# An attention and two-MLP kernel: one weight tile converted at each step of the second phase, low parts on VectorE

## The chip, the cores and the metric

The kernel runs on one core of a Trainium2 chip. A core has TensorE (PE; its weight loads are shown as PEld), VectorE (DVE), ScalarE (ACT), GpSimd (POOL) and SyncE (SP), which here only issues DMAs. The metric is the device time of one execution in microseconds (us), the median of several runs.

## What is computed

```python
def _attn_ref(q, k, v, s):                      # q, k, v: 4 x 8 x 576 x 64
    scores = scale * np.matmul(q, k.transpose(0, 1, 3, 2))
    bias = -(cum[:, :, :, None] - cum[:, :, None, :])
    scores = np.where(causal, -1000000000.0, scores + np.minimum(bias, 0.0))
...
    return np.matmul(attn, v).astype(np.float32)

def _moe_ref(x, w_in, w_out):                   # 2304 tokens, 512 x 2048, 2048 x 512
    h = x @ w_in
    g = h - np.tanh(h)
    return (g @ w_out).astype(np.float32)

def _moe2_ref(x, w1, w2, w3, w_out):            # 512 x 1024 (two), 1024 x 1024, 1024 x 512
    a = x @ w1
    b = x @ w2
    h = a * b @ w3
    return (h @ w_out).astype(np.float32)
```

The output of each function is the input of the next. The weights arrive as the bit patterns of float64 numbers, two 32-bit words each, and the kernel makes float32 of them itself.

## The kernel before, in words

Every product is computed from split operands. `split` (L61 to L63) makes a high part, a float32r cast of the source, and a low part, source minus high part. `mm3` (L96 to L100) then issues three matmuls for a piece of 128 rows: high by high, high by low, low by high. The high part is by default a copy on ScalarE (L62), the low part a subtraction on GpSimd (L63), unless the caller names another engine.

A weight tile is loaded raw (`load_raw`, L65, 512 KB, a pool of two buffers) and converted by `convert` (L72): three VectorE instructions put float32 words together from the halves (L76, L78, L80, into one of two `cvt` buffers), then `split` writes the tile's two halves.

The program has three phases. In the first, attention runs beside the first half of the first MLP (`ffn`), whose partial sums go to DRAM (`yp_d`). The second phase is the place of the change. `ffn_rest` goes through the tokens in five blocks (512, 512, 512, 512 and 256). For each block it splits x (`load_split`, four column groups, high parts on ScalarE, low parts alternately on GpSimd and VectorE), loads `yp`, and then takes f from 8 to 15: 12 matmuls hb = w_in[f] by x, tanh on ScalarE (thb), a subtraction on VectorE (thb again, L669), a split into ghb (ScalarE) and glb (VectorE), and `add_y` for the f before, 12 matmuls yb into four banks that stay for the whole block. At the block's end VectorE adds `yp` and writes xy (L679).

At the end of each f, `step()` advances the generator `w3_times_wout` once. There are 40 such steps. The generator prepares what the third phase needs. It converts eight tiles of `w_out2` (wo2, one at each step), and then for each f of eight: two tiles of w3 at a step each, the product w3o[f] = w3[f] by wo2 (24 matmuls), its split and its store at a third step, and at a fourth the two tiles w1[f] and w2[f], which are converted and stored ("parked") in `wg_d`. The park buffer is single. Names in the trace: w0_f and w1_f (written w_f where numbers are left out) are the tiles of w1 and w2. The third phase fetches w1, w2 and w3o from DRAM and computes the output.

The order in which each engine executes is not the written one here. A scheduler orders the instructions of each engine by its own model; the first phase's TensorE order alone is fixed by hand. Each engine, and SP's queue, then runs strictly in that order, so whatever stands behind a waiting instruction waits too.

Of the kernel before, what the change touches and what calls it, by code (L numbers as in the profile page):

```python
# [8 lines left out]
F32 = mybir.dt.float32  # L9
F32R = mybir.dt.float32r  # L10
# [5 lines left out]
P = 128  # L16
# [3 lines left out]
DM = 512  # L20
# [3 lines left out]
NG = 8  # L24
# [13 lines left out]
def tile_kernel(ctx: ExitStack, tc: tile.TileContext, qk, v, s, w_in, w_out, w1, w2, w3t, w_o2, outT):  # L38
    nc = tc.nc
# [21 lines left out]
    def split(dst_hi, dst_lo, src, hi=None, lo=None):  # L61
        (hi or nc.scalar.copy)(dst_hi, src)  # L62
        (lo or nc.gpsimd.tensor_sub)(dst_lo, src, dst_hi.bitcast(F32))  # L63
# [8 lines left out]
    def convert(raw, name, w=None):  # L72
# [10 lines left out]
        split(w[:, 0, :], w[:, 1, :], t.bitcast(F32))  # L83
# [526 lines left out]
    with ExitStack() as bctx:  # L610
# [4 lines left out]
        def convert_b(src, name, w=None):  # L615
            return convert(load_raw(src, name), name, w)

# [8 lines left out]
        def w3_times_wout(wt):  # L626
            wo2 = []

            for m in range(NG):
                wo2.append(convert_b(w_o2[m], f"wo2_{m}", wt.tile([P, 2, DM], F32R, tag="wo2", name=f"wo2_{m}", bufs=NG)))  # L630
                yield
            for f in range(NG):
                w3 = []
                for z in range(2):
                    w3.append(convert_b(w3t[f, :, 4 * z:4 * z + 4].rearrange("p m c -> p (m c)"), f"w3_{f}_{z}",
                                        wt.tile([P, 2, DM], F32R, tag="w3", name=f"w3_{f}_{z}", bufs=2)))
                    yield
                ps = ps_h.tile([P, 512], F32, tag="h", name=f"w3o{f}")
                for m in range(NG):
                    mm3(ps, w3[m // 4], P * (m % 4), wo2[m][:, 0, :], wo2[m][:, 1, :], m == 0, m == NG - 1)  # L640
                o = wt.tile([P, 2, DM], F32R, tag="w3o", name=f"w3o_{f}", bufs=1)
                split(o[:, 0, :], o[:, 1, :], ps, lo=nc.vector.tensor_sub)
                nc.sync.dma_start(w3o_d[f], o.bitcast(F32))
                yield
                for z, w in ((0, w1), (1, w2)):
                    park(load_raw(w[f], f"w{z}_{f}"), f"w{z}_{f}", wg_d[2 * f + z])
                yield

        def ffn_rest(step):
            for bi, (c0, n) in enumerate(blocks):  # L650
                xs = load_split(c0, n, "x")
# [9 lines left out]
                for f in range(F1, NF):  # L661
# [14 lines left out]
                    step()  # L676
                add_y(*prev)
# [87 lines left out]
```

## Time and profile before

| what | value |
|---|---|
| median of 3 runs | 1024.68 us |
| lowest and highest run | 1024.36, 1027.38 us |
| the profiled execution's own time | 1030.51 us |
| its span (first to last instruction) | 1028.2 us |
| mean granted clock of TensorE | 0.972 |
| the second phase's hb matmuls, first and last start | 417.0, 725.5 us |
| DMA bytes moved | 123.64 MB |

The profile is one execution. Its page gives the busy time of each engine over the whole span; other views cut it into stretches, show each engine's instructions in order of time with the idle time before them and what ended it, sum up who waited for whom, and follow the chain of work that ended last backwards. PEclk is the clock that TensorE was granted, as a share of 2.4 GHz. TensorE's matmuls overlap by design, so a row's time of one matmul (0.39 us) is longer than the distance between two starts.

### The profile page before, as it was taken

To read this page: it belongs to the slowest core of one execution; us is meant where nothing else is said; L and a number is where in the kernel's file an instruction comes from. 1 tells how busy PE (TensorE), PEld (TensorE's weight loads), DVE (VectorE), ACT (ScalarE), POOL (GpSimd) and SP (SyncE) were. 2 spreads that over 40 slices of the span, in tenths; PEclk is the share of its full clock that TensorE was granted. 3 is DMA by queue.
4 is the path that set the end of the run, shared out by engine and by line. 5 is a ranking of instruction groups with operands and counts; after the bars stand their busy time and mean duration, and the time that the engine had idled before them with its cause. 6 is when DMAs were issued, how large, how long until landed. Compare 5 with 4: busy or idle time off the path is not lost.

```text
span 1028.2 us, 15378 instructions
## 1 busy us (share of the span) xinstructions
PE 974.8 (95%) x5809; PEld 795.6 (77%) x5809; DVE 524.5 (51%) x1173; ACT 394.7 (38%) x978; POOL 253.8 (25%) x249
## 2 busy tenths in 40 slices
PE   5877898999999999999988999999999999999998
PEld 2544676668787878999867878889888888888898
DVE  8885645755656664642696575657312213122121
ACT  2555566676666654311432333232212112121121
POOL 3332565654433330100332322232101001000000
PEclk7879899999999999999998999999999999999999
DMA  6656745652222310135358361629800101001010
GB/s 201 205 184 231 237 148 175 207 205 83 94 73 99 106 67 31 62 101 186 118 164 272 103 221 61 211 101 341 335 1 1 41 1 41 1 1 42 1 41 21
DMA packets 46234, 123.64 MB, mean 120 GB/s; under 512 B 4977, under 2 KB 16913, under 8 KB 46161
## 3 DMA queue, kind: packets, MB, share of 16 engines
q1 hardware_dynamic: 41840, 106.94, 30.6%
q10 hardware_dynamic: 4320, 15.73, 4.6%
q8 instruction: 45, 0.74, 0.3%
q14 instruction: 29, 0.23, 0.1%
HBM read 92.09 MB, written 30.56 MB: 119 GB/s over the span
## 4 chain that ended last, share of the span: by engine, by line
PE 49%; DVE 6%; DMA 3%; ACT 1%; issue 1%; POOL 0%; SPq 0%; ACTq 0%; POOLq 0%; DVEq 0%
PE oc L100 10%; PE a L100 10%; PE b L100 10%; PE hb L100 6%; PE yb L100 6%; PE w3o L100 4%; PE h L100 2%; PE y L402 2%; DVE cvt_w L78 1%; DVE glb L63 1%; DVE x L63 1%; DMA raw_w<-in_w3t 1%; DVE cvt_w L76 1%; DMA win<-wf_d 1%; DVE cvt_wo L78 1%
## 5 line engine op out<-in xcount | busy, mean ns | idle before, releaser
L100 PEld LDWEIGHTS h<-xhl,win 128*128 128x128 f32 x864 | 111.5, 193 | 30.7 <-issue 12.6
L100 PE MATMUL h<-xhl,win 128*128 128x256 f32 x864 | 126.8, 293 | 8.5 <-DVE th L433 7.1
L712 DVE TENSOR_TENSOR pc<-b,pc 128x512 f32<-128x512 f32 (+1 forms) x40 | 25.5, 637 | 163.3 <-PE b L100 163.3
L100 PE MATMUL hb<-x,win 128*128 128x512 f32 (+1 forms) x480 | 106.8, 369 | 1.5 <-DMA win<-wf_d 1.5
L100 PE MATMUL a<-y,w 128*128 128x512 f32 (+1 forms) x480 | 106.4, 368 | 0.0
L100 PE MATMUL b<-y,w 128*128 128x512 f32 (+1 forms) x480 | 106.0, 368 | 0.0
L100 PE MATMUL yb<-ghb,wout 128*128 128x512 f32 (+1 forms) x320 | 99.1, 376 | 5.6 <-ACT ghb L62 3.7
L100 PEld LDWEIGHTS hb<-x,win 128*128 128x128 f32 x480 | 84.5, 189 | 17.0 <-DMA win<-wf_d 1.7
L100 PE MATMUL oc<-phc,w3s 128*128 128x512 f32 (+1 forms) x320 | 96.7, 368 | 0.0
L100 PEld LDWEIGHTS b<-y,w 128*128 128x128 f32 x480 | 84.3, 189 | 15.0
L100 PEld LDWEIGHTS a<-y,w 128*128 128x128 f32 x480 | 84.2, 189 | 14.9
L180 POOL TENSOR_SCALAR pr<-cb,cq 128x384 f32<-128x384 f32 (+1 forms) x48 | 86.2, 1813 | 9.5 <-DMA cb<-cum_d 5.7
L402 PE MATMUL y<-gh,wout 128*128 128x256 f32 x576 | 88.1, 292 | 0.0
L402 PEld LDWEIGHTS y<-gh,wout 128*128 128x128 f32 x576 | 74.7, 191 | 6.5 <-issue 5.1
L261 ACT ACTIVATE pr<-pr,nm 128x128 f32<-128x128 f32 (+2 forms) x120 | 71.4, 598 | 20.5 <-DVE nm L239 20.1
L63 POOL TENSOR_TENSOR y<-xy,y 128x512 fp32r<-128x512 f32 (+1 forms) x10 | 13.5, 1356 | 248.8 <-ACT y L62 248.6
L711 ACT COPY pc<-a 128x512 f32<-128x512 f32 (+1 forms) x40 | 21.8, 544 | 134.8 <-PE a L100 134.8
L100 PEld LDWEIGHTS yb<-ghb,wout 128*128 128x128 f32 x320 | 59.6, 192 | 17.8 <-ACT ghb L62 4.3
L201 PE MATMUL s_B<-qk 64*96 64x512 f32 (+2 forms) x256 | 60.2, 531 | 12.2 <-ACT pr L257 6.7
L100 PEld LDWEIGHTS oc<-phc,w3s 128*128 128x128 f32 x320 | 58.5, 189 | 9.9
L100 PE MATMUL yb<-glb,wout 128*128 128x512 f32 (+1 forms) x160 | 59.7, 377 | 1.7 <-DVE glb L63 1.7
L62 ACT CAST phc<-pc 128x512 fp32r<-128x512 f32 (+1 forms) x40 | 23.1, 578 | 93.2 <-DVE pc L712 93.2
(129 smaller groups left out, 1646.6 us busy)
## 6 DMA issues: line engine op xcount, KB each, us to landing
qk<-in_qk SPq DMA_DIRECT2D x16, 576.0 KB
raw_w<-in_w3t SPq DMA_DIRECT2D x16, 512.0 KB
raw_w<-in_w SPq DMA_DIRECT2D x16, 512.0 KB
wg_d<-park_w SPq DMA_DIRECT2D x16, 512.0 KB
w<-wg_d SPq DMA_DIRECT2D x16, 512.0 KB
raw_win<-in_w_in ACTq DMA_DIRECT2D x15, 512.0 KB
raw_wout<-in_w_out ACTq DMA_DIRECT2D x15, 512.0 KB
cb<-cum_d SPq DMA_DIRECT2D x12, 576.0 KB
```

The lines of the kernel that those rows point to most:

```text
L62: (hi or nc.scalar.copy)(dst_hi, src)
L63: (lo or nc.gpsimd.tensor_sub)(dst_lo, src, dst_hi.bitcast(F32))
L76: nc.vector.tensor_scalar(out=t, in0=r3[:, :, 1], scalar1=3, scalar2=0x3FFFFFFF, op0=ALU.logical_shift_left, op1=ALU.bitwise_and)
L78: nc.vector.scalar_tensor_tensor(out=t, in0=r3[:, :, 0], scalar=29, in1=t, op0=ALU.logical_shift_right, op1=ALU.bitwise_or)
L100: nc.tensor.matmul(ps, a, b, start=first and n == 0, stop=last and n == 2, skip_group_check=skip)
L180: nc.gpsimd.tensor_scalar(out=t[:pw, e, :w], in0=p.cb[:pw, e, :w], scalar1=c, scalar2=0.0, op0=ALU.add, op1=ALU.min)
L201: latest[0] = nc.tensor.matmul(ps[e][:PW[i], o:o + k1 - k0], x[:, 0, CH0[i]:CH0[i] + PW[i]], x[:, 1, k0:k1], start=(i, k0, k1, o) == UNITS ...
L261: nc.scalar.activation(t[:pw, :], t[:pw, :], AF.Exp, bias=m, scale=-1.0, accum_out=p.sums[:pw, e, c:c + 1])
L402: nc.tensor.matmul(o, wout[f][:, z, P * c:P * c + P], x, start=f == 0 and n == 0 and c % 2 == 0, stop=f == F1 - 1 and n == 2, skip_group_c ...
L711: nc.scalar.copy(t[:, :n], pa[:, :n])
L712: nc.vector.tensor_mul(t[:, :n], pb[:, :n], t[:, :n])
```

## The change

Four edits, all in the second phase. The low parts of all 40 weight tiles go from GpSimd to VectorE. The two parked tiles of an f get a step each, and w3o's product shares a step with the first of them, so that every step converts one tile. Two loads are issued ahead of the first step, and each step issues the load of the tile two further on, behind its own conversion. A store is issued at the beginning of the step after the one that made its data. Besides, the split of the next block's x is written ahead of the block's last `add_y`.

```diff
-    def convert(raw, name, w=None):
+    def convert(raw, name, w=None, lo=None):
...
-        split(w[:, 0, :], w[:, 1, :], t.bitcast(F32))
+        split(w[:, 0, :], w[:, 1, :], t.bitcast(F32), lo=lo)
...
         def w3_times_wout(wt):
-            wo2 = []
-
-            for m in range(NG):
-                wo2.append(convert_b(w_o2[m], f"wo2_{m}", wt.tile([P, 2, DM], F32R, tag="wo2", name=f"wo2_{m}", bufs=NG)))
+
+            todo = [(w_o2[m], f"wo2_{m}") for m in range(NG)]
+            for f in range(NG):
+                todo += [(w3t[f, :, 4 * z:4 * z + 4].rearrange("p m c -> p (m c)"), f"w3_{f}_{z}") for z in range(2)]
+                todo += [(w[f], f"w{z}_{f}") for z, w in ((0, w1), (1, w2))]
+            raws = [load_raw(*todo[m]) for m in range(2)]
+            store = []
+            wo2, w3 = [], []
+            for m, (_, name) in enumerate(todo):
+                while store:
+                    nc.sync.dma_start(*store.pop())
+                f, z = divmod(m - NG, 4)
+                if m < NG:
+                    w = wt.tile([P, 2, DM], F32R, tag="wo2", name=name, bufs=NG)
+                    wo2.append(w)
+                elif z < 2:
+                    w = wt.tile([P, 2, DM], F32R, tag="w3", name=name, bufs=2)
+                    w3.append(w)
+                else:
+                    w = cv.tile([P, 2, DM], F32R, tag="park", name=f"park_{name}", bufs=1)
+                    store.append((wg_d[2 * f + z - 2], w.bitcast(F32)))
+                convert(raws.pop(0), name, w, lo=nc.vector.tensor_sub)
+                if m + 2 < len(todo):
+                    raws.append(load_raw(*todo[m + 2]))
+                if m >= NG and z == 2:
+                    ps = ps_h.tile([P, 512], F32, tag="h", name=f"w3o{f}")
+                    for g in range(NG):
+                        mm3(ps, w3[g // 4], P * (g % 4), wo2[g][:, 0, :], wo2[g][:, 1, :], g == 0, g == NG - 1)
+                    w3 = []
+                    o = wt.tile([P, 2, DM], F32R, tag="w3o", name=f"w3o_{f}", bufs=1)
+                    split(o[:, 0, :], o[:, 1, :], ps, lo=nc.vector.tensor_sub)
+                    store.append((w3o_d[f], o.bitcast(F32)))
                 yield
-            for f in range(NG):
-                w3 = []
-                for z in range(2):
-                    w3.append(convert_b(w3t[f, :, 4 * z:4 * z + 4].rearrange("p m c -> p (m c)"), f"w3_{f}_{z}",
-                                        wt.tile([P, 2, DM], F32R, tag="w3", name=f"w3_{f}_{z}", bufs=2)))
-                    yield
...
-                nc.sync.dma_start(w3o_d[f], o.bitcast(F32))
-                yield
-                for z, w in ((0, w1), (1, w2)):
-                    park(load_raw(w[f], f"w{z}_{f}"), f"w{z}_{f}", wg_d[2 * f + z])
-                yield
+            while store:
+                nc.sync.dma_start(*store.pop())
...
+            xs = load_split(*blocks[0], "x")
             for bi, (c0, n) in enumerate(blocks):
-                xs = load_split(c0, n, "x")
...
                     step()
+                if bi + 1 < len(blocks):
+                    xs = load_split(*blocks[bi + 1], "x")
                 add_y(*prev)
```

The scheduler turns this into other orders. In the names, the number behind thb, ghb or glb is the block's first token and then f; the last number counts buffers. VectorE at the end of the first block, before:

```order
L63 TENSOR_TENSOR glb0_14_6169<-thb0_14_6165,ghb0_14_6168 128x512
L78 SCALAR_TENSOR_TENSOR cvt_wo2_7_6232<-raw_wo2_7_6230,cvt_wo2_7_6232 128x512
L80 SCALAR_TENSOR_TENSOR cvt_wo2_7_6232<-raw_wo2_7_6230,cvt_wo2_7_6232 128x512
L669 TENSOR_TENSOR thb512_8_6285<-hb512_8_6272,thb512_8_6285 128x512
L76 TENSOR_SCALAR cvt_w3_0_0_6295<-raw_w3_0_0_6293 128x512
L78 SCALAR_TENSOR_TENSOR cvt_w3_0_0_6295<-raw_w3_0_0_6293,cvt_w3_0_0_6295 128x512
L80 SCALAR_TENSOR_TENSOR cvt_w3_0_0_6295<-raw_w3_0_0_6293,cvt_w3_0_0_6295 128x512
L63 TENSOR_TENSOR glb0_15_6214<-thb0_15_6210,ghb0_15_6213 128x512
```

and after the change, at the same place:

```order
L63 TENSOR_TENSOR glb0_14_6173<-thb0_14_6169,ghb0_14_6172 128x512
L78 SCALAR_TENSOR_TENSOR cvt_wo2_7_6234<-raw_wo2_7_6154,cvt_wo2_7_6234 128x512
L63 TENSOR_TENSOR wo2_6_6188<-cvt_wo2_6_6189,wo2_6_6188 128x512
L80 SCALAR_TENSOR_TENSOR cvt_wo2_7_6234<-raw_wo2_7_6154,cvt_wo2_7_6234 128x512
L680 TENSOR_TENSOR thb512_8_6289<-hb512_8_6276,thb512_8_6289 128x512
L76 TENSOR_SCALAR cvt_w3_0_0_6297<-raw_w3_0_0_6195 128x512
L63 TENSOR_TENSOR wo2_7_6233<-cvt_wo2_7_6234,wo2_7_6233 128x512
L78 SCALAR_TENSOR_TENSOR cvt_w3_0_0_6297<-raw_w3_0_0_6195,cvt_w3_0_0_6297 128x512
L63 TENSOR_TENSOR glb0_15_6218<-thb0_15_6214,ghb0_15_6217 128x512
```

Two low parts of wo2 come in between, and one L80 goes behind glb0_15.

ScalarE and, below it, SP in the second block, around thb512_11, before:

```order
L62 CAST ghb512_10_6358<-thb512_10_6355 128x512
L62 CAST w3o_0_6399<-w3o0_6374 128x512
L62 CAST w3_1_1_6528<-cvt_w3_1_1_6531 128x512
L62 CAST park_w0_1_6632<-cvt_w0_1_6633 128x512
L668 ACTIVATE thb512_11_6416<-hb512_11_6403 128x512
L62 CAST ghb512_11_6419<-thb512_11_6416 128x512
```

```order
L67 DMA raw_w3_1_0_6488<-in_w3t 128x1024
L89 DMA wg_d_77<-park_w0_0_6437 128x1024
L653 DMA yp512_6266<-yp_d_74 128x4x512
L93 DMA w1_0_7922<-wg_d_77 128x1024
L67 DMA raw_w3_1_1_6529<-in_w3t 128x1024
L67 DMA raw_w0_1_6630<-in_w1 128x1024
L89 DMA wg_d_77<-park_w1_0_6447 128x1024
```

and after the change:

```order
L62 CAST ghb512_10_6362<-thb512_10_6359 128x512
L62 CAST park_w1_0_6449<-cvt_w1_0_6450 128x512
L62 CAST w3_1_0_6491<-cvt_w3_1_0_6492 128x512
L62 CAST w3o_0_6412<-w3o0_6387 128x512
L679 ACTIVATE thb512_11_6428<-hb512_11_6415 128x512
L62 CAST w3_1_1_6532<-cvt_w3_1_1_6533 128x512
L62 CAST ghb512_11_6431<-thb512_11_6428 128x512
L62 CAST park_w0_1_6573<-cvt_w0_1_6574 128x512
```

```order
L664 DMA yp512_6270<-yp_d_74 128x4x512
L67 DMA raw_w3_1_0_6385<-in_w3t 128x1024
L634 DMA wg_d_77<-park_w0_0_6378 128x1024
L67 DMA raw_w3_1_1_6456<-in_w3t 128x1024
L93 DMA w1_0_7922<-wg_d_77 128x1024
L67 DMA raw_w0_1_6498<-in_w1 128x1024
L634 DMA wg_d_77<-park_w1_0_6449 128x1024
```

The tanh moved in front of two high parts, and on SP the load of yp in front of a raw load; the raw loads keep their order.

VectorE at the end of the second block, where the x of the next blocks is split, before:

```order
L63 TENSOR_TENSOR x1024_3_6675<-xy_71,x1024_3_6675 128x512
L76 TENSOR_SCALAR cvt_w1_2_6860<-raw_w1_2_6857 128x512
L78 SCALAR_TENSOR_TENSOR cvt_w1_2_6860<-raw_w1_2_6857,cvt_w1_2_6860 128x512
L669 TENSOR_TENSOR thb512_15_6611<-hb512_15_6598,thb512_15_6611 128x512
L80 SCALAR_TENSOR_TENSOR cvt_w1_2_6860<-raw_w1_2_6857,cvt_w1_2_6860 128x512
L63 TENSOR_TENSOR x1536_1_7081<-xy_71,x1536_1_7081 128x512
L63 TENSOR_TENSOR glb512_15_6615<-thb512_15_6611,ghb512_15_6614 128x512
```

and after the change:

```order
L76 TENSOR_SCALAR cvt_w1_2_6862<-raw_w1_2_6756 128x512
L63 TENSOR_TENSOR park_w0_2_6790<-cvt_w0_2_6791,park_w0_2_6790 128x512
L78 SCALAR_TENSOR_TENSOR cvt_w1_2_6862<-raw_w1_2_6756,cvt_w1_2_6862 128x512
L63 TENSOR_TENSOR x1024_3_6662<-xy_71,x1024_3_6662 128x512
L76 TENSOR_SCALAR cvt_w3_3_0_6904<-raw_w3_3_0_6797 128x512
L680 TENSOR_TENSOR thb512_15_6623<-hb512_15_6610,thb512_15_6623 128x512
L80 SCALAR_TENSOR_TENSOR cvt_w1_2_6862<-raw_w1_2_6756,cvt_w1_2_6862 128x512
L63 TENSOR_TENSOR x1536_1_7068<-xy_71,x1536_1_7068 128x512
L78 SCALAR_TENSOR_TENSOR cvt_w3_3_0_6904<-raw_w3_3_0_6797,cvt_w3_3_0_6904 128x512
L63 TENSOR_TENSOR glb512_15_6627<-thb512_15_6623,ghb512_15_6626 128x512
```

The two x parts stand ahead of thb512_15 and glb512_15 in both; x1024_3 now comes two rows later.

## Rows read from the trace of the kernel before

**Rows 1.** The page: span, busy time and share of each engine.

```profile
span 1028.2 us, 15378 instructions
PE 974.8 (95%) x5809; PEld 795.6 (77%) x5809; DVE 524.5 (51%) x1173; ACT 394.7 (38%) x978; POOL 253.8 (25%) x249
```

**Rows 2.** Stretches: us; PE, PEld, DVE, ACT, POOL busy; PEclk, DMA share, GB/s.

```profile
510.00:520.00 10.00, 10.00 (x45) 8.07 (x43) 9.50 (x13) 3.50 (x6) 3.98 (x4) 1.00 0.38 122
520.00:530.00 10.00, 8.32 (x35) 6.41 (x35) 9.86 (x12) 3.48 (x6) 3.74 (x3) 1.00 0.49 154
...
550.00:560.00 10.00, 6.97 (x21) 5.30 (x20) 7.62 (x11) 2.97 (x6) 3.34 (x3) 0.73 0.81 260
...
600.00:610.00 10.00, 10.00 (x46) 8.28 (x45) 7.41 (x11) 3.55 (x6) 4.07 (x4) 1.00 0.66 231
```

**Rows 3.** Timeline, PE, its idle rows: start, us, what [idle before, releaser].

```profile
521.60 0.50 PE L100 MATMUL yb<-glb,wout 128*128 128x512 f32 x1 [1.45 <-DVE glb L63]
...
526.89 0.50 PE L100 MATMUL yb<-glb,wout 128*128 128x512 f32 x1 [0.23 <-DVE glb L63]
...
534.13 0.50 PE L100 MATMUL yb<-ghb,wout 128*128 128x512 f32 x1 [1.24 <-DVE xy L679]
...
555.23 1.65 PE L100 MATMUL yb<-ghb,wout 128*128 128x512 f32 x3 [3.03 <-ACT ghb L62]
...
593.45 0.47 PE L100 MATMUL yb<-ghb,wout 128*128 128x512 f32 x1 [0.59 <-ACT thb L668]
...
693.88 1.21 PE L100 MATMUL yb<-ghb,wout 128*128 128x512 f32 x4 [0.69 <-ACT ghb L62]
```

**Rows 4.** Stretch of 2 us behind the longest idle time, columns as before.

```profile
557.00:559.00 2.00, 2.00 (x6) 1.52 (x6) 1.53 (x3) 0.99 (x2) 0.29 (x1) 0.50 0.53 184
```

**Rows 5.** The chain of waits, 535 to 635 us: start, us, what.

```profile
538.97 7.34 DMA raw_w<-in_w3t
...
548.32 3.42 DMA raw_w<-in_w
...
555.23 5.49 PE yb L100 x12
560.72 2.45 PE hb L100 x9
...
568.61 2.72 PE yb L100 x12
...
585.19 4.88 DMA wg_d<-park_w
...
616.40 2.04 PE hb L100 x9
```

**Rows 6.** Timeline, DVE, from the end of the first block.

```profile
500.64 1.50 DVE L76 TENSOR_SCALAR cvt_wo<-raw_wo 128x512 uint32<-128x512 uint32 x1 [1.19 <-POOL wo L63]
...
522.18 0.69 DVE L80 SCALAR_TENSOR_TENSOR cvt_wo<-raw_wo,cvt_wo 128x512 uint32<-128x512 uint32 x1
522.79 0.68 DVE L669 TENSOR_TENSOR thb<-hb,thb 128x512 f32<-128x512 f32 x1
523.39 0.42 DVE L76 TENSOR_SCALAR cvt_w<-raw_w 128x512 uint32<-128x512 uint32 x1
523.84 1.67 DVE L78 SCALAR_TENSOR_TENSOR cvt_w<-raw_w,cvt_w 128x512 uint32<-128x512 uint32 x1
...
530.97 1.78 DVE L78 SCALAR_TENSOR_TENSOR cvt_w<-raw_w,cvt_w 128x512 uint32<-128x512 uint32 x1
```

**Rows 7.** Timeline, POOL, one low part of that stretch.

```profile
523.61 1.35 POOL L63 TENSOR_TENSOR wo<-cvt_wo,wo 128x512 fp32r<-128x512 f32 x1 [2.61 <-ACT wo L62]
```

**Rows 8.** Groups by line, DVE, 495 to 740 us: busy us, mean ns, idle before.

```profile
L63 DVE TENSOR_TENSOR w3o<-w3o,w3o 128x512 fp32r<-128x512 f32 x8 | 5.5, 690 | 4.7 <-ACT w3o L62 4.7
```

**Rows 9.** Waits, who for whom: us in total, times, longest.

```profile
ACT park_w L62 <- DMA wg_d<-park_w: 22.3, 6, 4.5
...
SPq L67 <- DVE cvt_w L80: 56.4, 25, 5.6
```

More of the change, by code (lines that the diff above doesn't have):

```diff
@@ L613, in tile_kernel @@
         ps_y = bctx.enter_context(tc.tile_pool(name="ps_yb", bufs=1, space=PSUM))
-        def convert_b(src, name, w=None):
-            return convert(load_raw(src, name), name, w)
         def load_split(c0, n, name):
@@ L626, in w3_times_wout @@
         def w3_times_wout(wt):
-            wo2 = []
-            for m in range(NG):
-                wo2.append(convert_b(w_o2[m], f"wo2_{m}", wt.tile([P, 2, DM], F32R, tag="wo2", name=f"wo2_{m}", bufs=NG)))
-                yield
-            for f in range(NG):
-                w3 = []
-                for z in range(2):
-                    w3.append(convert_b(w3t[f, :, 4 * z:4 * z + 4].rearrange("p m c -> p (m c)"), f"w3_{f}_{z}",
-                                        wt.tile([P, 2, DM], F32R, tag="w3", name=f"w3_{f}_{z}", bufs=2)))
-                    yield
[L638 to L642, printed above, removed]
-                nc.sync.dma_start(w3o_d[f], o.bitcast(F32))
-                yield
-                for z, w in ((0, w1), (1, w2)):
-                    park(load_raw(w[f], f"w{z}_{f}"), f"w{z}_{f}", wg_d[2 * f + z])
-                yield
+            todo = [(w_o2[m], f"wo2_{m}") for m in range(NG)]
```

## The prediction, made before the change was run

> **What bounds the kernel now.** The page says where to look: TensorE is busy for 95% of the span, VectorE for 51%, GpSimd for 25% [rows 1]. So time can be won only where TensorE stands still or runs at its lower clock; elsewhere the other engines are cover. Next come stretches of 10 us. Where nothing disturbs the second phase, TensorE is busy for 10.00 of 10 us at a granted clock of 1.00 and VectorE for 7.41; between 510 and 530 us VectorE is at 9.50 and 9.86, and TensorE falls to 8.32; in 550 to 560 us it has 6.97, at a clock of 0.73 [rows 2]. The timeline of TensorE names the holes, in the rows that carry an idle time and a releaser: 1.45, 0.23, 1.24, 3.03, 0.59 and 0.69 us, together **7.23 us**, all released by VectorE or ScalarE, none by a DMA directly [rows 3].
>
> The longest hole has a tail. After it the granted clock is 0.50, the 1.2 GHz level [rows 4]. The chain of waits prices it: the 12 yb matmuls behind the hole take 5.49 us and the 9 hb matmuls after them 2.45 us; the same counts take 2.72 and 2.04 us elsewhere in that chain [rows 5]. The tail costs 5.49 + 2.45 - 2.72 - 2.04 = **3.18 us**. The profiled execution thus holds 7.23 + 3.18 = 10.41 us that this change could reach. Everything else on the path is matmuls, whose number doesn't change.
>
> Why the holes are there: the VectorE rows start 0.60 us apart (0.34 to 0.45 for L76) where nothing disturbs them, though the L78 at 523.84 takes 1.67 us, while GpSimd's low part of 523.61 runs for 1.35 us [rows 6, 7]. Nine VectorE instructions between 500.64 and 530.97 are stretched so, each beside one GpSimd low part; the first takes 1.50 and the last 1.78 us, where 0.42 and 0.69 is usual [rows 6]. They stand in front of the glb and xy that TensorE waits for in the first three holes. The fourth hole ends a chain of two loads, 7.34 and 3.42 us, with a thb and a ghb queued behind the conversions [rows 5].
>
> **The change, part by part.**
>
> *Low parts on VectorE.* 40 subtractions move. Their price there is unseen. The nearest row is w3o's low part, 8 of them at 690 ns mean [rows 8], in its step 0.60 us by the spacing of the thb and L80 rows [rows 6]; a low part with both inputs in SBUF beside GpSimd's x could be stretched as far as the 1.78 us of the last row there. I take 0.60, because after the change GpSimd has only the x parts left. Up to the xy of the first block, nine of the 40 are added: 9 x 0.60 = 5.4 us. Nine stretches go, each 1.0 to 1.1 us by the first, the 523.84 and the last row [rows 6]: some 9 us. Net, VectorE is some 3.6 us earlier at glb0_15, and the first three holes, 2.92 us together, close. Past that point VectorE needs, per step, L76 0.34 to 0.45, L78, L80, low part, thb and glb at 0.60: about 3.4 us. TensorE needs 24 matmuls, twice the 2.72 us of a row of 12 [rows 5], or 5.44 us, and 24 more for w3o at every fourth step. VectorE is covered.
>
> *One tile at each step, loads two ahead.* There are 40 steps and 40 tiles either way; what goes is the step with two tiles. The raw pool still has two buffers, so a load waits for the L80 of the tile two before it. It does so already: SP's loads wait for that L80 25 times, 56.4 us in all [rows 9]. The order of the loads on SP is the same in the order shown above, and yp (1 MB) now stands in front of raw_w3_1_0 instead of behind it. I price the loads at no gain by themselves; they come earlier only as VectorE does. Their cover is the distance from one L80 to the L76 two tiles on: at TensorE's pace two steps of 5.44 us less a tile's own 1.6 us, some 9 us on average, where a load took 3.42 to 7.34 us [rows 5].
>
> *Where the long hole was.* On ScalarE the tanh thb512_11 stood behind two high parts, w3_1_1 and park_w0_1, and so behind their conversions. It now stands in front of both. That is the piece most likely to remove the 3.03 us, and with it the 3.18 us of slow clock. Bounds: 0, if the thb on VectorE stays late behind L80 of w3_1_1, and 6.21 us.
>
> *Stores a step later.* Sixteen wg_d stores and eight w3o_d stores stay on SP. Before, the store whose landing took 4.88 us was queued behind a load [rows 5]; now it is issued ahead of the load of the tile after it. ScalarE waited for such landings 6 times, 22.3 us in all [rows 9]. The same buffer is still single, so the wait stays, and VectorE's low part of the second parked tile now shares it: see the rivals. At the end of the phase none of the last stores comes later among the fetches of phase three: nothing.
>
> *The next block's x split sooner.* In the order above x1024_3 and x1536_1 stood ahead of thb512_15 and glb512_15 already; they move by two or three rows. This edit alone is worth nothing. The 0.59 and 0.69 us holes at the block changes close for the other reason: four VectorE instructions in front of thb512_15 are stretched now, by two x parts and two low parts; two remain, and 2.1 us less stretch stands against two added low parts, 1.2 us. Bounds of this part: 0 to 1.28 us.
>
> **Sum.** Against the profiled execution: 1030.51 - 10.41 = 1020.10 us. The median of the unprofiled runs is 1024.68, 5.83 us below that execution, and the three runs spread over 3.02 us (1024.36 to 1027.38). That spread is as large as the slow-clock tail, and the median lies at its low end, so I do not count the tail in an unprofiled run, only the idle time: 1024.68 - 7.23 = **1017.4 us**. If the tail is there too, 1014.3; if besides the wait on a load is not there, 1024.68 - 4.20 = 1020.5.
>
> **Rivals.**
>
> *Loads too late* (0.17). yp ahead of raw_w3_1_0 and the two loads behind it keep thb512_11 waiting, and the 3.03 us hole stays where it is. For it: the 7.34 us load, taken with the same yp in flight. Against it: the tanh's new place and some 3.6 us of lead. The other five holes close: 1024.68 - 4.20 = 1020.5 us.
>
> *A store's landing takes VectorE* (0.13). park_w1_f's low part waits on VectorE for its high part, and that for the landing of park_w0_f's store; in front of the GpSimd queue this cost nothing, on VectorE thb and glb stand behind it. 22.3 us over 6 waits is 3.7 us each; the slack per step is 5.44 - 3.4 = 2.0 us, so each wait that is met in full costs 1.7 us. Three of eight give 5.1 back: 1024.68 - 7.23 + 5.1 = 1022.6 us. It decides if the store is issued less than 4.88 us ahead of that cast.
>
> *VectorE becomes the bound* (0.07, slower). If the stretched rows are long for a reason other than GpSimd, moving work onto an engine that is busy for 9.86 of 10 us adds nine low parts at 0.69 us, 6.2 us, to the first three holes; a hole that long brings a tail like the 3.18 us, and the other three holes, 4.31 us, close: 1024.68 + 6.2 + 3.18 - 4.31 = 1029.8 us. The point is glb0_14 later than 521.60 us. The Trainium skill, page "Perfetto Trace Analysis", section "Optimizing Scalar/DVE Operations", says that offloading from a saturated VectorE to ScalarE or even GpSimd may make sense, which speaks against this change; the same section doubts it between VectorE and GpSimd, as they share a read port. By its first half this rival's time would come; by its second, the forecast. The row at 523.84 beside the one at 523.61 sides with the second, so the chance is small.
>
> *Nothing that counts* (0.11). Unprofiled runs hold few of these holes, or new small waits replace them: 1022 to 1025.5, taken as 1024 us.
>
> **Chances.** The forecast has 0.52. A measurement of this kernel can tell about 0.3%, or 3.1 us, from no change; faster means below 1021.6 us. That takes in the forecast (0.52), the late loads (0.17), and the mild half of the store rival and of the last (0.10): 0.79 faster. The rest of these, 0.14, is the same, and VectorE as the bound is slower, 0.07. For the range I go down to 1013.4, the forecast with the tail and a little more, and up to 1022.6, the store rival; outside lie the slower rival and most of the last.
>
> **What would show it.** Right: no GpSimd low part but x and y between 490 and 730 us; L78 and L80 means near 690 ns; TensorE idle below 1.5 us from 494 us to the end of the phase, clock 1.00 throughout; hb 8 of the first block and everything before it where it was. Wrong: an idle time over 1 us in front of a yb. With a load named behind it, the first rival; with the landing of wg_d<-park_w, the second; with L78 still near 900 ns, the third. If the holes are gone and the time hardly moves, the sum was made from holes that only the profiled execution had.

## The result, and the profile after

The changed kernel takes 1018.34 us (median of 4 runs, 1016.88 to 1019.15). The kernel before, run beside it, takes 1026.03 us (4 runs, 1024.36 to 1028.14). The ratio is 0.9917, with a 95% interval of 0.9896 to 0.9939: faster, by 7.7 us in the medians, or 0.8%; the whole interval lies below 1. The forecast was 1017.4 us, in a range of 1013.4 to 1022.6.

The page of the changed kernel, part 1, answers to [rows 1]. VectorE is no busier than before (524.5 us there), although it executes 40 instructions more. GpSimd has lost 57 us.

```profile
PE 970.3 (95%) x5806; PEld 794.6 (78%) x5809; DVE 521.4 (51%) x1213; ACT 395.1 (39%) x978; POOL 196.5 (19%) x209
```

The same stretches as in [rows 2], same columns:

```profile
510.00:520.00 10.00, 10.00 (x46) 8.29 (x45) 9.29 (x18) 5.03 (x9) 0.00 (x0) 1.00 0.49 157
520.00:530.00 10.00, 10.00 (x46) 8.29 (x45) 9.86 (x18) 3.94 (x7) 0.00 (x0) 1.00 0.49 157
...
550.00:560.00 10.00, 9.60 (x42) 7.43 (x40) 7.69 (x14) 3.70 (x7) 0.00 (x0) 1.00 0.66 221
```

TensorE is full where it had 8.32, and has 9.60 where it had 6.97; the clock of 0.73 is gone. VectorE shows how a busy share can mislead: 9.86 of 10 us in 520 to 530 us before and after, but 18 instructions now where 12 were. GpSimd does nothing there. The clock was 1.00 through the whole phase.

Two idle rows of TensorE are left in the phase, against the six of [rows 3]; all six are gone:

```profile
555.56 0.50 PE L100 MATMUL yb<-glb,wout 128*128 128x512 f32 x1 [0.40 <-DVE glb L63]
...
560.36 0.50 PE L100 MATMUL yb<-glb,wout 128*128 128x512 f32 x1 [0.17 <-DVE glb L63]
```

Where the time came from is read best from the first start of yb (early in the second phase) to the first start of a (third phase). One group of matmuls, in the view of a tile: line, count, shortest/median/longest ns, first and last start. First the kernel before:

```profile
L100 PE MATMUL yb<-ghb,wout x320: 277/389/795, 497.0 to 733.6; 128*128 128x512 f32 x128, 128*128 128x256 f32 x32
L100 PE MATMUL a<-y,w x480: 278/389/397, 727.1 to 1019.8; 128*128 128x512 f32 x128, 128*128 128x256 f32 x32
```

And the changed kernel:

```profile
L100 PE MATMUL yb<-ghb,wout x320: 278/389/397, 497.2 to 722.5; 128*128 128x512 f32 x128, 128*128 128x256 f32 x32
L100 PE MATMUL a<-y,w x480: 278/389/397, 715.9 to 1008.6; 128*128 128x512 f32 x128, 128*128 128x256 f32 x32
```

The first phase ends at the same time in both (497.0 and 497.2), and the a matmuls take 292.7 us in both. The second phase falls from 727.1 - 497.0 = **230.1** to 715.9 - 497.2 = **218.7 us**: all 11.4 us of the profiled executions lie in it. Below, "second phase" means this distance.

VectorE from 520.33 us in the changed kernel, to be laid beside [rows 6]; the L63 wo row is one of the low parts that came over:

```profile
520.33 0.68 DVE L63 TENSOR_TENSOR wo<-cvt_wo,wo 128x512 fp32r<-128x512 f32 x1
520.93 0.69 DVE L78 SCALAR_TENSOR_TENSOR cvt_w<-raw_w,cvt_w 128x512 uint32<-128x512 uint32 x1
521.53 0.69 DVE L63 TENSOR_TENSOR glb<-thb,ghb 128x512 fp32r<-128x512 f32 x1
522.13 0.69 DVE L80 SCALAR_TENSOR_TENSOR cvt_w<-raw_w,cvt_w 128x512 uint32<-128x512 uint32 x1
522.73 0.43 DVE L76 TENSOR_SCALAR cvt_w<-raw_w 128x512 uint32<-128x512 uint32 x1
523.07 0.69 DVE L680 TENSOR_TENSOR thb<-hb,thb 128x512 f32<-128x512 f32 x1
```

Every row is 0.60 us behind the last (0.34 for L76), the low part too; none is stretched to 1.5 or 1.8 us.

### The profile page after: what moved, and what is told of

It reads as the page before. It is cut to its first block, busy times and chain, and to the rows that moved or that the text cites. A ratio compares the mean times of both kernels' runs of the same rounds, so it can differ in the third digit from the quotient of the medians.

```text
span 1017.0 us, 15372 instructions
## 1 busy us (share of the span) xinstructions
PE 970.3 (95%) x5806; PEld 794.6 (78%) x5809; DVE 521.4 (51%) x1213; ACT 395.1 (39%) x978; POOL 196.5 (19%) x209
## 4 chain that ended last, share of the span: by engine, by line
PE 74%; DMA 10%; DVE 8%; ACT 4%; issue 2%; POOL 0%; SPq 0%; ACTq 0%; DVEq 0%
PE oc L100 10%; PE a L100 10%; PE b L100 10%; PE h L100 9%; PE hb L100 8%; PE y L402 8%; PE yb L100 6%; PE pv L298 4%; PE w3o L100 4%; PE s_B L201 3%; DMA cb<-cum_d 2%; DMA raw_wout<-in_w_out 2%; PE pt_B L272 2%; DMA raw_w<-in_w3t 2%; DMA raw_win<-in_w_in 1%
## 5 line engine op out<-in xcount | busy, mean ns | idle before, releaser
L100 PE MATMUL yb<-ghb,wout 128*128 128x512 f32 (+1 forms) x320 | 96.1, 368 | 0.0
L63 POOL TENSOR_TENSOR x<-xy,x 128x512 fp32r<-128x512 f32 (+1 forms) x10 | 14.1, 1423 | 289.9 <-ACT x L62 289.8
L201 PE MATMUL s_B<-qk 64*96 64x512 f32 (+2 forms) x256 | 58.1, 516 | 11.0 <-ACT pr L257 6.5
L63 POOL TENSOR_TENSOR y<-xy,y 128x512 fp32r<-128x512 f32 (+1 forms) x10 | 13.3, 1334 | 281.3 <-ACT y L62 281.1
```

Of the source, the lines that this page charges most:

```text
L100: nc.tensor.matmul(ps, a, b, start=first and n == 0, stop=last and n == 2, skip_group_check=skip)
L201: latest[0] = nc.tensor.matmul(ps[e][:PW[i], o:o + k1 - k0], x[:, 0, CH0[i]:CH0[i] + PW[i]], x[:, 1, k0:k1], start=(i, k0, k1, o) == UNITS ...
```

## The experiments

Each run is compared with the kernel before on the same chip. The second phase of its profiled execution stands beside the time, since the first phase, at which no edit but e8's is aimed, ends anywhere from 492.9 to 498.0 us (first yb).

| kernel | median, us | ratio to before, 95% | first yb, us | second phase, us |
|---|---|---|---|---|
| before | 1026.03 | | 497.0 | 230.1 |
| changed | 1018.34 | 0.9896 to 0.9939 | 497.2 | 218.7 |
| e1, low parts alone | 1015.30 | 0.9859 to 0.9913 | 492.9 | 220.0 |
| e2, all but the low parts | 1028.43 | 0.9991 to 1.0030 | 495.3 | 230.7 |
| e3, changed + GpSimd dummy 128x512 | 1026.96 | 0.9987 to 1.0032 | 493.2 | 228.7 |
| e4, before again | 1026.74 | 0.9985 to 1.0015 | 498.0 | 229.4 |
| e5, changed again | 1020.39 | 0.9903 to 0.9957 | 496.2 | 219.2 |
| e6, changed + third raw buffer | 1013.69 | 0.9854 to 0.9888 | 493.5 | 217.7 |
| e7, changed + x and y low parts on VectorE | 1015.73 | 0.9878 to 0.9910 | 495.0 | 218.4 |
| e8, changed + first phase's low parts on VectorE | 1019.67 | 0.9908 to 0.9947 | 498.0 | 219.4 |
| e9, changed + GpSimd dummy 128x256 | 1021.52 | 0.9916 to 0.9957 | 495.1 | 223.0 |
| e10, e6 with the low parts on GpSimd | 1027.59 | 0.9986 to 1.0027 | 494.3 | 228.3 |
| e11, e6 and e7 together | 1013.12 | 0.9835 to 0.9882 | 493.8 | 217.5 |

The theory at this point: GpSimd's low parts hold VectorE up, and that is where the holes come from. The rival: the new order on ScalarE and TensorE (the tanh ahead of two high parts) makes the gain, and with it the steps, loads and stores.

### e1: the low parts alone

```diff
-            return convert(load_raw(src, name), name, w)
+            return convert(load_raw(src, name), name, w, lo=nc.vector.tensor_sub)
...
-                    park(load_raw(w[f], f"w{z}_{f}"), f"w{z}_{f}", wg_d[2 * f + z])
+                    park(load_raw(w[f], f"w{z}_{f}"), f"w{z}_{f}", wg_d[2 * f + z], lo=nc.vector.tensor_sub)
```

> The kernel before with one edit of the four: the low parts of the second phase's 40 tiles on VectorE, with the old loop, the old loads, the old stores and the old place of the x split. Its instructions stand on every engine in the same order and with the same waits as in the changed kernel. Both theories (GpSimd's reads stretch VectorE; the new order on ScalarE and TensorE is what counts) expect the time of the changed kernel, 1017 to 1019.5 us, a ratio of 0.990 to 0.994. If loading two steps ahead, the later store or the sooner x split is worth anything beyond what the order shows, it is slower by that: 1020 us or more.

Measured: 1015.30 us, ratio 0.9886 (0.9859 to 0.9913), second phase 220.0 us. The median lies below the expected 1017 us, and 3.0 us below that of the changed kernel in the first comparison; but the first phase of its profile was 4.3 us shorter (492.9 against 497.2), while its second was 1.3 us longer. In the two traces the instructions of VectorE, ScalarE, GpSimd and SP stand in the same order. The whole gain comes from the one edit.

### e2: all the rest, without the low parts

```diff
-                convert(raws.pop(0), name, w, lo=nc.vector.tensor_sub)
+                convert(raws.pop(0), name, w)
```

> The changed kernel with the low parts back on GpSimd: one tile at each step, loads two ahead, stores a step later and x sooner all stay. Its instructions stand on every engine in the order of the kernel before. Both theories expect the time of the kernel before, a ratio of 0.998 to 1.002, and the holes of the first block back: glb0_15 again behind some nine stretched VectorE rows, L78 and L80 at about 905 ns. If the loop's new form is worth something, the ratio is under 0.997.

Measured: 1028.43 us, ratio 1.0011 (0.9991 to 1.0030), second phase 230.7 us, and six idle rows of TensorE of 1.39, 0.20, 1.25, 3.29, 0.65 and 0.68 us: those of [rows 3] again. One tile at each step, loads two ahead, later stores and the sooner x, without the low parts, are worth nothing, because the scheduler makes the old order of them.

### e3 and e9: the contention given back, in two doses

```diff
                 convert(raws.pop(0), name, w, lo=nc.vector.tensor_sub)
+                idle = wt.tile([P, DM], F32, tag="idle", name=f"idle_{name}", bufs=1)
+                nc.gpsimd.tensor_sub(idle, w[:, 0, :].bitcast(F32), w[:, 0, :].bitcast(F32))
```

> The changed kernel, with one subtraction of 128x512 more on GpSimd for each of the 40 tiles of the second phase, of the high part from itself into a scratch tile: the low parts' traffic on GpSimd comes back, while VectorE, ScalarE and SyncE keep the changed kernel's order; the output is the same. Theory A, GpSimd's reads of SBUF stretch VectorE: L78 and L80 rise from 721 and 685 ns towards 900, some nine rows before glb0_15 are stretched by about 1 us each, and as VectorE now also does the low parts, TensorE stands idle for 5 us or more in the first block: 1023 to 1030 us. Theory B, the new order alone gives the gain: L78 may be stretched, but no hole over 1 us comes back: 1017 to 1020 us.

Measured: 1026.96 us, ratio 1.0010 (0.9987 to 1.0032), second phase 228.7 us. In the trace VectorE and ScalarE keep the changed kernel's order, and no engine waits for a dummy. A result that nobody reads takes back 10.0 of the 11.4 us. TensorE's holes return, some at other places (three of seven rows):

```profile
500.49 0.50 PE L100 MATMUL yb<-glb,wout 128*128 128x512 f32 x1 [0.76 <-DVE glb L63]
523.88 0.50 PE L100 MATMUL yb<-glb,wout 128*128 128x512 f32 x1 [0.99 <-DVE glb L63]
...
544.11 0.50 PE L100 MATMUL yb<-glb,wout 128*128 128x512 f32 x1 [2.70 <-DVE glb L63]
```

So the order alone is not the gain. Behind the hole of 2.70 us the granted clock fell here too, so a part of the 10.0 us is slow clock:

```profile
540.00:550.00 10.00, 7.30 (x26) 5.50 (x25) 6.91 (x10) 2.23 (x4) 2.57 (x2) 0.83 0.73 272
```

Nor is this the kernel before again: VectorE here does the low part itself and is held besides. The run shows that GpSimd's traffic is enough for a loss of this size; how the loss divides in the kernel before is another question. L78's mean rose to 812 ns only, less than the 900 that I expected; other rows (L76 to 679, the park_w low part to 1087 ns) took their share. The time lay within the expected range, the size of the stretch did not: 0.86 us a row and not 1 us. For one pair, the GpSimd row and then the VectorE row beside it:

```profile
517.45 1.04 POOL L647 TENSOR_TENSOR idle_wo<-wo 128x512 f32<-128x512 f32 x1 [3.16 <-ACT wo L62]
```

```profile
517.50 1.53 DVE L78 SCALAR_TENSOR_TENSOR cvt_wo<-raw_wo,cvt_wo 128x512 uint32<-128x512 uint32 x1
518.96 0.68 DVE L63 TENSOR_TENSOR wo<-cvt_wo,wo 128x512 fp32r<-128x512 f32 x1
```

The next row starts 1.46 us later and not 0.60. Then with half the width:

```diff
-                nc.gpsimd.tensor_sub(idle, w[:, 0, :].bitcast(F32), w[:, 0, :].bitcast(F32))
+                nc.gpsimd.tensor_sub(idle[:, :256], w[:, 0, :256].bitcast(F32), w[:, 0, :256].bitcast(F32))
```

> The dummy subtraction on GpSimd of the earlier run at half the width, 128x256: VectorE and ScalarE keep the order of that run and of the changed kernel, the output is the same. If VectorE is held for as long as GpSimd reads, the stretch of a VectorE row beside it falls from 0.86 us (row spacing of 1.46 against 0.60) to about half, the holes of the first block go, and the second phase (first yb to first a matmul: 218.7 us in the changed kernel, 228.7 with the full dummy) takes 219 to 223 us, in all some 1018 to 1021 us. If the stretch is a fixed price for each GpSimd instruction, it stays at 0.86 and the time at 1025 to 1028 us.

Measured: 1021.52 us, ratio 0.9936 (0.9916 to 0.9957), second phase 223.0 us. The pair of the same two instructions:

```profile
516.98 0.61 POOL L647 TENSOR_TENSOR idle_wo<-wo 128x256 f32<-128x256 f32 x1 [3.49 <-ACT wo L62]
```

```profile
517.03 1.10 DVE L78 SCALAR_TENSOR_TENSOR cvt_wo<-raw_wo,cvt_wo 128x512 uint32<-128x512 uint32 x1
518.06 0.68 DVE L63 TENSOR_TENSOR wo<-cvt_wo,wo 128x512 fp32r<-128x512 f32 x1
```

Spacing 1.03 us, a stretch of 0.43 for a GpSimd row of 0.61; with the full width 0.86 for one of 1.04. In both VectorE's row starts 0.05 us behind GpSimd's and ends 0.54 us behind its end. The median lies 0.5 us above the expected time, the second phase at the upper end of its range. No hole is left in the first block, as expected; three are left behind it (1.10, 0.64 and 0.37 us, at 540.98 to 550.54) and one of 0.56 us at 707.40. Without dummy, with half and with the full one, the second phase takes 218.7, 223.0 and 228.7 us. The clock stayed at 1.00 with the half dummy, so the step to the full one holds the slow clock as well. That is the dose and its effect.

### e4 and e5: each kernel again

> The kernel before, unchanged, for its clock and its holes run by run: a ratio of 0.999 to 1.001. If the stretch of half clock in 557 to 559 us belongs to the kernel, it is in this profile too, behind a hole of about 3 us; if it was chance, this profile has the hole and a clock of 1.00, and is nearer to the median of 1024 to 1026 us.

Measured: 1026.74 us, ratio 1.0000. The slow stretch is in this profile and in that of e2, whose order is the same. The stretch of 550 to 560 us, e4 first, then e2; columns as in [rows 2]:

```profile
550.00:560.00 10.00, 7.23 (x25) 5.48 (x24) 8.37 (x12) 3.47 (x6) 4.20 (x3) 0.83 0.78 274
```

```profile
550.00:560.00 10.00, 6.71 (x18) 4.97 (x17) 8.04 (x12) 2.89 (x6) 2.56 (x2) 0.66 0.81 263
```

Three profiles of this order hold the slow clock behind the long hole (2.77, 3.03 and 3.29 us of idle time: 0.83, 0.73 and 0.66). In these executions it comes with this order.

> The changed kernel, unchanged, beside the runs of the next three on one chip: 1015 to 1018.5 us, a ratio of 0.988 to 0.993 to the kernel before. It holds what the low parts alone gave (0.9886); a ratio below 0.986 or above 0.994 would say that the other three edits count for something after all.

Measured: 1020.39 us, ratio 0.9930 (0.9903 to 0.9957), second phase 219.2 us. The median lies above the 1018.5 us that I expected, and the six runs go from 1014.14 to 1022.97 us. With the four of the first comparison and the four of e1, the same order of instructions has now run 14 times, from 1014.14 to 1022.97 us, with a median of 1017.4. The three profiles differ by 4.3 us at the end of the first phase and by 1.3 us in the second. What moves the first phase was not looked into.

### e6 and e10: a third raw buffer

```diff
-    def load_raw(src, name, queue=nc.sync, pin=False):
-        raw = cv.tile([P, 2 * DM], U32, tag="raw", name=f"raw_{name}")
+    def load_raw(src, name, queue=nc.sync, pin=False, pool=None):
+        raw = (pool or cv).tile([P, 2 * DM], U32, tag="raw", name=f"raw_{name}")
...
             raws = [load_raw(*todo[m]) for m in range(2)]
+            raws.append(load_raw(*todo[2], pool=wt))
...
-                if m + 2 < len(todo):
-                    raws.append(load_raw(*todo[m + 2]))
+                if m + 3 < len(todo):
+                    raws.append(load_raw(*todo[m + 3], pool=wt if m % 3 == 2 else None))
```

> The changed kernel with a third buffer for raw tiles in the second phase, out of the phase's own pool, and the loads three steps ahead in place of two. If two buffers are what makes VectorE wait for loads (11 times, 13.2 us, for w3's tiles), those waits fall under 5 us, and the holes that are left at 552 to 561 us (0.57 us in the changed kernel, 1.65 us with the low parts alone) close: 0.5 to 2 us faster than the changed kernel, a ratio of 0.987 to 0.991. If the DMA engines' rate or yp's load sets the landing, the waits stay over 10 us and the time too.

Measured: 1013.69 us, ratio 0.9871 (0.9854 to 0.9888), second phase 217.7 us, and no idle row of TensorE in it. The idle time of VectorE ahead of L76 on w's tiles, most of it waits for loads, first in the changed kernel, then in this one (busy, mean ns, idle before and its releasers):

```profile
L76 DVE TENSOR_SCALAR cvt_w<-raw_w 128x512 uint32<-128x512 uint32 x32 | 16.6, 520 | 15.3 <-DMA raw_w<-in_w3t 13.2 <-DMA raw_w<-in_w 1.7
```

```profile
L76 DVE TENSOR_SCALAR cvt_w<-raw_w 128x512 uint32<-128x512 uint32 x32 | 16.3, 516 | 2.3 <-DMA raw_w<-in_w3t 1.9
```

15.3 us fall to 2.3. In the changed kernel a wait of this kind stands on VectorE in front of the glb of each of the two holes that the change left:

```profile
553.88 0.43 DVE L76 TENSOR_SCALAR cvt_w<-raw_w 128x512 uint32<-128x512 uint32 x1 [1.27 <-DMA raw_w<-in_w3t]
...
558.55 0.43 DVE L76 TENSOR_SCALAR cvt_w<-raw_w 128x512 uint32<-128x512 uint32 x1 [0.63 <-DMA raw_w<-in_w3t]
```

With the third buffer both holes are gone. But the scheduler also gave VectorE and ScalarE another order in the first two blocks, so the buffer is not separated from the order. In the second phase the two are worth 1.0 us against the first profile of the changed kernel and 1.5 against e5's, as expected. The medians of e5 and e6 are 6.7 us apart, which is more than the 0.5 to 2 us expected. Of the rest the first phase of the two profiles accounts for 2.7 us (493.5 against 496.2); what remains is not placed.

With the low parts back on GpSimd, by the edit of e2:

> The third raw buffer and the loads three steps ahead, with the low parts on GpSimd as in the kernel before. If the contention is the cause, the loads alone help the one hole that ends a chain of loads (3.03 us with its slow clock, 5 to 6 us in all) at most, and the holes at glb and xy in the first block (1.45, 0.23, 1.24 us) stay: a second phase of 224 to 230 us and 1019 to 1026 us. If late loads were what cost the time, it does as well as the kernel with the third buffer and the low parts on VectorE: 217.7 us and 1014 us.

Measured: 1027.59 us, ratio 1.0007 (0.9986 to 1.0027), second phase 228.3 us. The median is above the expected range, the second phase within it. Eight idle rows, among them:

```profile
525.62 0.50 PE L100 MATMUL yb<-glb,wout 128*128 128x512 f32 x1 [1.54 <-DVE glb L63]
...
552.65 1.21 PE L100 MATMUL yb<-ghb,wout 128*128 128x512 f32 x4 [2.24 <-ACT ghb L62]
```

The better loads take only some of the long hole (2.24 us, and the clock stays at 1.00 behind it). VectorE's waits for loads of w's tiles, 5.8 us in the kernel before, are all gone here, and the time is not (the order differs a little from the kernel before here as well). Late loads were not what cost most of the time.

### e7 and e11: the last low parts of GpSimd

```diff
-                split(x[:, 0, :n], x[:, 1, :n], xy[:, c, c0:c0 + n], lo=nc.vector.tensor_sub if c % 2 else None)
+                split(x[:, 0, :n], x[:, 1, :n], xy[:, c, c0:c0 + n], lo=nc.vector.tensor_sub)
```

> The changed kernel with the low parts of the second phase's x tiles and of y on VectorE too, the last that GpSimd does there (ten parts of 1.35 us mean). No hole of the changed kernel stands beside one of them, so taking the last contention away is worth nothing: within 0.2% of the changed kernel, with x and y low parts on VectorE near 690 ns and VectorE's rows beside them no longer over 1 us. If contention were still on the path, it is 1 us or more faster.

Measured: 1015.73 us, ratio 0.9894 (0.9878 to 0.9910), second phase 218.4 us, 0.3 us below the changed kernel's. The x parts of 128x512 are at 685 ns mean, y at 683. The median lies 4.7 us below e5's on the same chip, outside the 0.2% that I expected and on the side of the rival; the second phase is 0.8 us below e5's, the first 1.2 us, and one profile does not place the rest. All four runs lie within the range of the 14 above, so these times do not show that x's contention costs anything, nor that it costs nothing. Both edits together:

> The third raw buffer together with the x and y low parts on VectorE, the two that were not slower than the changed kernel. With the third buffer alone TensorE has no idle row left in the second phase (217.7 us), so this should be worth nothing more there: a second phase of 217.5 to 218.5 us and a time within 0.2% of 1013.7 us, apart from what the first phase adds or takes (its end lies between 492.9 and 498.0 us in eight profiles). If it is faster by 2 us or more, x's contention still cost something on the path.

Measured: 1013.12 us, ratio 0.9859 (0.9835 to 0.9882), second phase 217.5 us, no idle row. Within 0.06% of e6. This version and e6 beat both kernels; between the two nothing can be told.

### e8: the same medicine for the first phase

```diff
-        split(w[:, 0, :], w[:, 1, :], t.bitcast(F32), lo=lo)
+        split(w[:, 0, :], w[:, 1, :], t.bitcast(F32), lo=lo or nc.vector.tensor_sub)
```

> The changed kernel with the low parts of the first phase's weight tiles (31, converted and parked ones) on VectorE as well. By the theory that a GpSimd low part costs VectorE 1.0 us where it costs 0.6 us to do it there, VectorE is some 12 us less busy up to 450 us; TensorE has holes there behind VectorE's th and the softmax steps, so the time falls by 2 to 8 us, a ratio of 0.983 to 0.989. The rival: in that phase VectorE is the busiest engine next to TensorE (0.78 of the first 200 us) and GpSimd's parts fall into its idle time, so 31 times 0.6 us is added to it: 1 to 10 us slower than the changed kernel.

Measured: 1019.67 us, ratio 0.9928 (0.9908 to 0.9947): neither, no difference to e5's 1020.39 us. The first 200 us in e5 and in e8, columns as in [rows 2] (VectorE's share is 0.69 there; the expectation's 0.78 is that of the first 100 us in the kernel before):

```profile
0.00:200.00 200.00, 163.16 (x1034) 112.12 (x1038) 137.65 (x349) 112.15 (x323) 92.74 (x105) 0.87 0.59 197
```

```profile
0.00:200.00 200.00, 158.89 (x1005) 108.72 (x1010) 147.09 (x382) 110.10 (x320) 54.41 (x71) 0.86 0.62 210
```

VectorE became 9.4 us busier, where I had expected it to be 12 us less busy. The price of 1.0 us for a GpSimd low part does not carry over: over the first 490 us VectorE's busy time rose by 6.4 us, from 297.0 to 303.4, for 32 low parts (four groups of 8, 23.2 us; the expectation said 31), so the stretch that went is about 23.2 - 6.4 = 16.8 us, an estimate of 0.53 for each part. It depends on what VectorE does beside GpSimd.

## Why the prediction was right, point by point

**The stretch of VectorE is GpSimd's doing** (the row at 523.84 beside the one at 523.61): shown. e3 and e9 bring stretch and holes back without touching VectorE's order, more of both for the longer GpSimd instruction. The rival "VectorE becomes the bound" needed another reason for the long rows; no run shows one.

**"Net, VectorE is some 3.6 us earlier at glb0_15."** The size is near, the count behind it is not. In the kernel before glb0_15 starts at

```profile
526.15 0.68 DVE L63 TENSOR_TENSOR glb<-thb,ghb 128x512 fp32r<-128x512 f32 x1
```

and in the changed kernel at 521.53, 4.6 us earlier, although the phase begins 0.2 us later. The term of 0.60 us for a low part was right to the row (rows of 0.60 us apart; means of 686 ns for w, 682 for wo and 745 for the parked ones). But I counted to the first xy: ahead of glb0_15 stand seven of the nine stretched rows, 7.75 us of stretch by the distances between starts, and eight of the nine low parts, 4.8 us. That gives 3.0 us and not 3.6. The rest is what I did not count: the L80 that went behind glb0_15, 0.60 us, and VectorE's idle time of 1.19 us at 500.64, behind a low part on GpSimd [rows 6]. Together they make 4.7 us, near what was measured; that the sum of 3.6 came close is luck.

That idle time is a second way in which GpSimd held VectorE: L76 needs a cvt buffer that GpSimd's low part still reads. In the kernel before, VectorE waits for it in the second phase once behind a low part of wo2 (the 1.19 us) and six times behind those of w3's tiles, here w (us in total, times, longest; then one of the six):

```profile
DVE cvt_w L76 <- POOL w L63: 20.2, 6, 4.7
```

```profile
574.97 0.43 DVE L76 TENSOR_SCALAR cvt_w<-raw_w 128x512 uint32<-128x512 uint32 x1 [4.69 <-POOL w L63]
```

I read the waits on loads and stores and left this row out. In the changed kernel it does not exist; e10 still has it. It looks larger than it is. All six waits stand at 574.97 us or later, behind the four holes that cost most, and the chain of waits of the kernel before passes through none of them. The only low part on GpSimd in that chain, from 498 us to the end of the phase, is the one behind the 1.19 us:

```profile
498.85 1.76 POOL wo L63
```

So on that chain the buffer costs this one wait, 1.19 us against 7.75 us of stretch ahead of glb0_15. No run takes away the one without the other.

**"The first three holes, 2.92 us together, close"; 0.59 and 0.69 "close for the other reason", less stretch:** all five did.

**"Where the long hole was":** closed, with its slow clock. I gave the credit to the tanh's new place on ScalarE. How much of it the place has is open: no run has the whole new place with the low parts on GpSimd, or the old place without them. e10 comes nearest: low parts on GpSimd, the tanh ahead of park_w0_1 but still behind w3_1_1; 2.24 us of the hole stay. e3 and e9 have the new place beside a dummy. In e3 TensorE loses 2.70 us one f earlier, in front of glb512_10 by the count of the yb matmuls, and nothing at ghb512_11; in e9 some of the hole is back at ghb512_11:

```profile
548.27 1.21 PE L100 MATMUL yb<-ghb,wout 128*128 128x512 f32 x4 [0.64 <-ACT ghb L62]
```

So the place alone does not keep this stretch free of holes.

**"I price the loads at no gain by themselves; they come earlier only as VectorE does."** Right for what the change does: e2 and e1. But the loads are the next thing late, as the two rows that remain and e6 show; the cover of "some 9 us on average" was too much for w3's tiles: VectorE waits for their loads 11 times, 13.2 us, and the two TensorE holes that are left follow such waits. The rival "Loads too late" was thus there in small: not the old hole but two others, 0.57 us (1.65 in e1, 0.73 in e5), where I gave it 3.03.

**"A store's landing takes VectorE":** no. Who waited for whom in the changed kernel, the second phase (us in total, times, longest):

```profile
ACT park_w L62 <- DMA wg_d<-park_w: 15.5, 6, 4.5
```

```profile
DVE park_w L63 <- ACT park_w L62: 4.8, 5, 1.8
```

ScalarE still waits 6 times [rows 9], and VectorE shares it for 4.8 us in all, 1.8 at the longest. The two holes that are left have a wait for a load on VectorE as the last one before them, not this one.

**"The next block's x split sooner": "This edit alone is worth nothing."** So it is, with the other two edits of the loop (e1 against the changed kernel, e2 against before).

**The sum: one term mis-sized.** From three profiles of each order, the second phase falls from 230.1 (230.1, 230.7, 229.4) to 219.3 us (218.7, 220.0, 219.2), by 10.8 us; the pair of the result by 11.4. I had 7.23 + 3.18 = 10.41 us, of which 0.57 us stayed, so 9.84 us to go. The idle column understates a hole: matmul rows are 0.39 us long but start 0.23 apart. The matmuls around the first hole:

```profile
519.76 0.39 PE L100 MATMUL hb<-x,win 128*128 128x512 f32 x1
521.60 0.50 PE L100 MATMUL yb<-glb,wout 128*128 128x512 f32 x1 [1.45 <-DVE glb L63]
521.94 0.39 PE L100 MATMUL yb<-ghb,wout 128*128 128x512 f32 x1
```

The second was due at 519.99; it came at 521.60, 1.61 us late, where the column says 1.45, and the third came 0.11 us more than a spacing later. That is 0.27 us for a hole; over six holes, estimated from this one, 1.6 us, which covers the difference.

**"I do not count the tail in an unprofiled run."** This choice gave 1017.4 us; with the tail it would have been 1014.3. The tail was in each of the three profiles of this order, two of them taken afterwards, so nothing in them speaks for leaving it out; whether every other execution had it is not shown. The differences of the medians measured side by side are 7.7, 10.9 and 6.2 us (result, e1, e5), which straddle both sums. They cannot decide, because the first phase alone moves by up to 5 us from profile to profile. That the median of 14 runs falls on 1017.4 us is partly luck.

## What to carry to other kernels

Look for long VectorE rows beside GpSimd rows before asking which engine has time to spare: here a low part on the idle GpSimd cost VectorE about 1.1 us (0.84 to 1.22 in the first block), and doing it there costs 0.60. Give a busy share its instruction count (9.86 of 10 us is 12 instructions in one kernel and 18 in the other), and test a suspected contention by giving it back as a dummy of two sizes with the order kept. Where a scheduler orders the instructions, compare the orders first: of this change only the low parts left a trace in it.

## What the runs showed of the hardware

The stretch has a shape: VectorE's row ends a fixed time behind GpSimd's. In the pairs of e3 and e9 GpSimd ends at 518.49 and 517.59 and VectorE at 519.03 and 518.13, 0.54 us later in both; in the kernel before the pair of [rows 6, 7] ends at 524.96 and 525.51, 0.55 us apart. The other stretched rows of 128x512 with two inputs in SBUF keep to 0.54 to 0.56 us in the traces of both kernels, e2, e3, e4, e9 and e10, and those of L76 to 0.28 or 0.29. So a row is held the longer, the longer GpSimd still has to go: by 0.43 us beside 0.61, by 0.86 beside 1.04.

Of the two-input rows it strikes those with both inputs in SBUF, and spares those that read one from PSUM. glb has thb and ghb in SBUF, thb reads hb from PSUM; first the kernel before, with GpSimd's low parts, then the changed kernel; busy and mean ns, 128x512 alone:

```profile
L63 DVE TENSOR_TENSOR glb<-thb,ghb 128x512 fp32r<-128x512 f32 x30 | 24.8, 828 | 13.2 <-ACT ghb L62 12.8
L669 DVE TENSOR_TENSOR thb<-hb,thb 128x512 f32<-128x512 f32 x28 | 19.1, 684 | 15.7 <-ACT thb L668 15.6
```

```profile
L63 DVE TENSOR_TENSOR glb<-thb,ghb 128x512 fp32r<-128x512 f32 x30 | 20.6, 687 | 11.0 <-ACT ghb L62 10.7
...
L680 DVE TENSOR_TENSOR thb<-hb,thb 128x512 f32<-128x512 f32 x28 | 19.2, 684 | 7.6 <-ACT thb L679 7.6
```

828 against 687 ns for glb; 684 and 684 for thb. Means alone do not tell whether thb ran beside GpSimd at all. xy, which reads yb from PSUM, did: in the kernel before two rows of it take 1.28 us beside a low part of 1.37, and they take the same 1.28 us at 529.64 in the changed kernel, with GpSimd idle:

```profile
534.21 1.37 POOL L63 TENSOR_TENSOR park_w<-cvt_w,park_w 128x512 fp32r<-128x512 f32 x1 [2.01 <-ACT park_w L62]
```

```profile
534.33 1.28 DVE L679 TENSOR_TENSOR xy<-yb,yp 128x512 f32<-128x512 f32 x2
```

The Trainium skill, page "SBUF — State Buffer", section "Who interferes with whom", states this: a VectorE instruction with two inputs in SBUF contends with a GpSimd instruction that reads SBUF, one with at most one such input does not, outside the two-port modes. The rows of glb, thb and xy agree. L76 reads one tile only, from SBUF, and is stretched all the same (1.50 us at 500.64 [rows 6], where 0.42 is usual); whether it runs in such a mode, no run here shows.
